# A new hand-written order for the engines of a fused attention and MLP kernel

## The chip, the cores and the metric

The kernel runs on one core of one Trainium2 chip. The core has five engines that run beside each other, each through its own list of instructions and in that list's order: PE (matrix products and their weight loads, PEld), DVE (vector arithmetic), ACT (functions by table, and copies), POOL (a second, slower vector engine, used here for casts and for issuing weight loads) and SP (which only issues transfers). Engines wait for each other by semaphores. Transfers between HBM and the on-chip memory are moved by 16 DMA engines; a transfer is issued by an engine's list and lands later.

The metric is the device time of one execution in microseconds. Three executions of the kernel before took 264.19, 266.99 and 267.23 us; the median is 266.99.

## The reference

Inputs are q, k and v of 4 batches, 8 heads, 768 positions and 64 columns, a list of 3 random key blocks for each of the 24 query blocks of 32, and the weights of an MLP.

```python
scores = q @ k.T / sqrt(64)                     # per batch and head, 768 x 768
mask   = |block_i - block_j| <= 1, or block_i or block_j is first or last,
         or block_j in sampled_blocks[block_i]
attn   = exp(where(mask, scores, -1e9) - max);  attn = attn / sum(attn)
x      = (attn @ v), heads side by side         # 3072 tokens x 512
h      = x @ w_in                               # 3072 x 2048
g      = h * sigmoid(beta * h)
out    = g @ w_out                              # 3072 x 512, float32
```

## The kernel before

**Attention.** Heads go in pairs (16 pairs, four in each batch), so that a pair's 2 x 64 columns fill 128 rows. Each pair's k, q and v are loaded as float32 into staging tiles `st` (the first pairs also into the not yet used `g` tiles), cast to float16 (`s16`, shown as `s` in the profile, and `va`), and k and q are transposed into `kX` and `qX`: for the first four pairs by PE and a copy, for the others by a transposing transfer that SP issues. The 768 queries of a pair are worked in two units of 256 and 512. A unit has several key steps: two 64-row matmuls for the two heads side by side give scores in PSUM (`sc`), ACT takes the exponential (`et`), DVE multiplies by the 0/1 mask. For the first four units PE adds the mask before the exponential instead. Then PE multiplies with v (`av`; a column of twos beside v gives twice the sum), DVE takes the reciprocal and normalizes into `xst`, and `xst` is transposed into `x`: by PE in the first eight units and the last, by a transposing transfer otherwise.

**MLP.** The tokens go in seven tiles: 256, five of 512, 256. For each of 16 chunks of the hidden width PE makes half of `h` (step kind `hp`; `x` is halved by the twos above), ACT `t = tanh(beta * h/2)` (`t_sb`), and DVE the product `(t + 1) * h/2` into `g`, which is h times the sigmoid. The second product is done plainly in the first tile. In the others it is done by seven half-sized products in place of eight; for that DVE makes sums of halves of `g` (`s`) and of `w_out` (`w_mix`), PE makes the seven products (`pr`), and ACT and DVE add them up in `osb`, from which SP stores to HBM.

**Tiles.** All tiles have fixed slots: 9 `st`, 7 `s16`, 15 `et`, 5 `xst`, 4 double PSUM banks, only 2 `osb` and 2 `g`. Whoever takes a slot waits for all that still use it.

**What sets the order.** The program first builds a list of steps (`Node`, numbered 0 to 1316 in the order of building), each with its engine or a choice of engines. The order in which they are emitted, and so each engine's list, is not found by a scheduler: it is written out in the string `STEPS` (line 43) and read by `in_steps` (line 163). A word such as `45G2` is step 45, on engine G (POOL; P is PE, A ACT, D DVE, S SP), in slot 2 of the tile that it takes. `824P2:823` emits step 824 crossed with step 823: both products are cut into upper and lower 64 rows, and PE runs the upper half of one beside the lower half of the other; the partner's own word later runs the other halves. `3x256V5` is three warm-up matmuls of 256 columns on zeros into bank 5. At the very start `emit_first` sets up constants and runs four warm-up matmuls of 512 columns.

A step on POOL that casts is also tied to the last DVE step ahead of it in the list (line 1034), so that it runs beside a DVE step that reads PSUM.

Steps that the texts below name: loads (`add_load`, line 497) of the first two pairs, 12, 16, 20, 24, 30, 34, 38 and 64, and of the next two, 44, 48, 54 and 58; their casts (`add_cast`, line 522); the mask steps 2, 3, 5, 7 and 9; the first scores, 91 to 95; step 310, the first `hp` of the second MLP tile; the stores (`add_store`, line 830) 395 to 398 of that tile; the transposes of attention tiles 593 to 723 and the first `hp` of the fourth tile, 724; the copy 566 into `osb` in the third tile.

Of the kernel before, what the change touches and what calls it, by code (L numbers as in the profile page):

```python
# [48 lines left out]
119P0 120A9 67D 98P 190P2 191A4 53D2 99D0 100D0 109P3 101P2 193P0 89P3 90D2 187P2 70P3 110P 102D  # L49
71D 194Ad 77G 78G 111Df 112D1 188Ae 196P0 199P1 197Aa 200A2 121P2 122P 123D1 124D4 195D 214P0  # L50
215A6 125P7 113P6 114D 202P2 203A5 126D 127P2 201D 198D 128A0 130P6 211P2 131A1 212A0 129D1 132D
189D 216D 136P3 145P7 146A1 137A3 133P2 134A5 213D 204D 142P0 143A4 147D 138D 144D 148P1 149A0
150D 135D 220P2 139P6 221Ab 140A2 151P7 217P2 152A6 141D 153D 192D 218Ac 219D 166P0 154P2 167A0
155A3 163P6 172P3 157P7 164A6 173A4 156D 168D 174D 226P2 165D 158A5 159D 160P2 227A3 169P3 223P0
161A1 228D 222D 170A3 171D 162D 224A8 252P2 225D 253A7 205P3 206P 207Df 208D2 246P0 254D 249P1
235G7 239G1 229P2:230 247A1 250Ad 261P3 262A9 230P 290P0 231D2 232D3 291Ab 181P23:175 258P3 255P2
256Ac 259A2 175P 209P1 182P 210A0 278P2 236S 243G2 248D 176P:183 237D5 263D 279Aa 281P0 284P3 240S
238S1 282A4 285A6 244S 270S3 183P 287P2 288Ae 177P 178P 184P 179A0 251D 257D 292D 260D 293P3 294A0
280D 241D2 358D 359D 360D 283D 289D 242S 265P0:264 185D1 286D 273S8 276S5 302S6 305S4 414P2 295D
362D 415A3 271G4 399P1 264P 266De 363D 267D4 405P3 296P2 297P 272S2 400A9 406Ac 268P3 298D7 299D0  # L60
269A 233P1 402P3 234A 300P0 403A2 411P1 408P2 274D0 308S0 422S7 425S1 412Aa 275S 301D 401D 310P0
322P7 331P2 319P1 311A6 364D 313P3 409Ab 332A0 303G3 320A1 323A4 314A5 277G2 423G5 309G0 328P5
329A3 306G6 361D 365D 316P6 312D1 407D 333D 321D 324D 315D 330D 317A1 413D 318D 430P0 431A1 404D
416D 432D 343P23:325 436P2 437A5 180S 304S3 186S 428S6 424S0 307S 325P 326A6 439P3 433P0 434A8
337P4 327D 435D 438D 410D 334P5 352P3 340P0 338A5 344A2 345D 335A0 353A1 346P1 354D 440A7 445P1
426G1 245G3 429G1 341A4 347A3 339D 336D 349P6 342D 446Ad 348D 442P2 366D0 447D 441D 443A4 444D
355P7 453P0 417P1 418P 456P2 454A0 356A6 350A5 419D3 420D1 427S 457Ac 459P0 460Ae 448P1:449 455D
357D 351D 369D 465P2 466A2 449P 468P3 469A6 462P0 463A8 375P4 450Dc 451D3 488P1 372P5:376 482P3
458D 467D 461D 464D 370D 470D 489A1 483A3 484D 367D 476P0 376P 477Aa 479P1 485P3 480Ab 373P 471P0
472P 486A4 586P1 587Ae 491P3 492Ad 374D1 377D 383P:380 473D3 474D0 583P0 594P1 595A5 608S8 380P  # L70
478D 381P:384 584Ac 481D 487D 368D 493D 490D 611S3 619P3 580P1 384P 620A6 609D4 378D 385A0 581A9
495P0:494 622P3 623A7 494P 616P1 379D 371D 617A0 614S5 630S0 633S2 612G6 634G5 389P 600P3 601A3
496D1 382D 497D2 386P:390 641P1 585D 596D 582D 631G2 638P0 642Aa 588D 390P 597P3 421S2 636S7 452S
652S1 475S 391D 610S1 644P1 387P 639A2 498S 653G0 621D 624D 388D 655S8 658S4 656G1 499P4 645A1
613S 598A8 395S 632S2 517P3 500A3 518A0 505P2 506A2 501D0 519D 589P0 590P 591D5 507D 392P4:508
592D4 646D 660P3 661A4 674S1 654S3 677S6 599D 675D3 618D 502P23:514 663P0 664Ab 508P 509A1 635S
396S 680S3 666P3 514P 665D 662D 510D 667Ad 515A2 503A0 526P0 527A6 511P1 393P 512A3 538P4 394A
539A4 678G4 516D 504D 688P3 682P1 689A9 528D 676S0 520P0 521A5 529P5 625P3 626P 683Ac 530A1 640D
540D 643D 602D 522D 627D5 513D 535P4 657S 628D0 536A2 696P1 699P0 603P3 604P 531D 684D 547D0 700Ae
605D2 537D 606D1 701D 679S 593S1 697A5 544P5 523P1 545A0 710P1 685P3 532P0 524A6 546D 711A6 647P2  # L80
659G3 615G0 668D 525D 541P2 533A4 534D 686A0 542A2 648P 702P0 637G2 669P3 670P 649Dh 650D3 703A3
808P2 543D 671D9 672D2 550D 687D 548D 698D 809A7 553P23:556 713P0 814P3 556P 557P:554 714Ad 815A4
716P2 717A8 690D 810D 551D 673S 398S 820P0 554P 555D1 681G1 704D 805P3 821A1 806Aa 691P2 692P
693D9 694D4 561P 817P3 818A0 706P2:705 828P0 558D 564P:562 829Ab 851S1 854S4 857S7 705P 559D 831P3
# [988 lines left out]
```

## Time and profile before

| what | us |
|---|---|
| median of three executions | 266.99 (264.19 to 267.23) |
| the profiled execution | 267.46 |
| its span, first to last instruction | 265.7 |
| PE busy | 254.4 |
| DVE busy | 227.4 |
| ACT busy | 213.1 |
| POOL busy | 41.7 |

The profile is of one execution. An engine's busy time counts its own instructions, not those that only wait or issue transfers. A row of the timeline starts with the start and the length in us and names engine, line, operation, what is written `<-` what is read, the shape and the number of instructions that the row merges; in brackets stand the idle time ahead of it and what ended that. Nearly all instructions have line L198, a helper that records them, so rows are told apart by their tiles. The chain of waits follows the end of the program back, at each step to what released it. The stage view gives for each stretch of time the busy time and number of instructions of each engine, the granted TensorE clock, the share of the DMA engines and what they moved.

### The profile page before, as it was taken

The numbers are of one execution on the slowest core, as the hardware profiler recorded it, in microseconds if no ns is written. First come the engines' busy times: TensorE is split into PE (matmuls) and PEld (weight loads), VectorE is DVE, ScalarE is ACT, GpSimd is POOL, SyncE is SP. The second block draws the span as 40 slices with busy tenths as digits, with TensorE's granted clock in tenths as the row PEclk, the third lists the DMA queues.
The fourth block names the chain that finished last, engine by engine and source line by source line (L and its number), as shares of the span: only waits on it lengthen the run. The fifth ranks groups of instructions, "written<-read, shape, count | busy, mean of one in ns | idle before, by whom it ended". The sixth has DMA issues, their size and how long they took to land.

```text
span 265.7 us, 8448 instructions
## 1 busy us (share of the span) xinstructions
PE 254.4 (96%) x3589; PEld 172.7 (65%) x3589; DVE 227.4 (86%) x442; ACT 213.1 (80%) x284; POOL 41.7 (16%) x60
## 2 busy tenths in 40 slices
PE   6999899999999999999989999989999999999994
PEld 1576575454357976558766557845757986568883
DVE  4475997989999997999988999999989997599581
ACT  3589999898999997999878999876689894574441
POOL 5183000017030051112104130060000000000000
PEclk9999999999999999999999999999999999999999
DMA  5899993899479449900965949640050100230042
GB/s 159 251 338 210 204 233 80 204 271 266 142 201 229 82 106 266 267 12 26 284 171 190 168 81 215 144 72 2 2 178 2 38 11 4 69 118 2 0 158 81
DMA packets 50153, 36.79 MB, mean 138 GB/s; under 512 B 29748, under 2 KB 46660, under 8 KB 50116
## 3 DMA queue, kind: packets, MB, share of 16 engines
q1 hardware_dynamic: 46368, 32.06, 47.2%
q0 software_dynamic: 3680, 4.19, 9.3%
q8 instruction: 28, 0.46, 0.7%
q14 instruction: 9, 0.07, 0.1%
q10 hardware_dynamic: 68, 0.01, 0.0%
HBM read 27.27 MB, written 6.29 MB: 126 GB/s over the span
## 4 chain that ended last, share of the span: by engine, by line
PE 72%; DVE 18%; ACT 4%; issue 2%; DMA 1%; SPq 0%; DVEq 0%; ACTq 0%
PE sc L198 72%; DVE et L198 6%; DVE g L198 6%; ACT et L198 3%; DVE s L198 1%; DMA out_dram<-osb 1%; DVE xst L198 1%; DVE w_out_sb L198 1%; DVE recip L198 1%; DVE kX L198 1%; DVE osb L198 1%; DVE va L198 1%; ACT t_sb L198 0%; ACT osb L198 0%; DVE w_mix L198 0%
## 5 line engine op out<-in xcount | busy, mean ns | idle before, releaser
L198 ACT ACTIVATE et<-sc 128x1024 f16<-128x1024 f32 x144 | 140.7, 1036 | 14.4 <-PE sc L198 11.8
L198 PE MATMUL sc<-x,w_in_sb 128*128 128x512 f16 (+2 forms) x496 | 92.8, 351 | 1.0 <-DVE g L198 1.0
L198 DVE TENSOR_TENSOR et<-et,mask 128x960 f16<-128x960 f16 x132 | 83.4, 668 | 0.7 <-ACT et L198 0.5
L198 ACT ACTIVATE t_sb<-sc,beta_c_sb 128x512 f16<-128x512 f32 (+1 forms) x112 | 65.4, 644 | 21.7 <-PE sc L198 16.7
L198 PEld LDWEIGHTS <-w_in_sb 128*128 128x128 f16 (+1 forms) x496 | 42.7, 97 | 38.3 <-issue 5.6
L198 DVE SCALAR_TENSOR_TENSOR g<-t_sb,sc 128x512 f16<-128x512 f16 (+1 forms) x112 | 63.1, 603 | 5.1 <-ACT t_sb L198 4.5
L198 PEld LDWEIGHTS <-g 64*128 64x128 f16 (+1 forms) x698 | 50.3, 96 | 16.7 <-issue 6.1
L198 PE MATMUL sc<-w_out_sb,g 64*128 64x256 f16 (+3 forms) x560 | 55.6, 280 | 1.6 <-ACT osb L198 1.6
L198 PE MATMUL sc<-qX,kX 64*128 64x512 f16 (+1 forms) x384 | 51.4, 329 | 0.8 <-DMA qX<-s 0.5
L198 PEld LDWEIGHTS <-et 64*128 64x128 f16 (+1 forms) x1608 | 41.0, 95 | 9.1 <-issue 3.2
L198 PE MATMUL sc<-va,et 64*128 64x65 f16 (+1 forms) x1608 | 44.1, 191 | 1.1 <-DVE xst L198 0.5
L198 POOL CAST s<-st 128x768 f16<-128x768 f32 (+1 forms) x23 | 20.4, 902 | 94.3 <-PE sc L198 48.6
L198 PEld LDWEIGHTS <-kX 64*128 64x128 f16 x384 | 19.9, 95 | 13.8 <-issue 8.2
L198 PEld LDWEIGHTS <-s 64*128 64x128 f16 (+1 forms) x320 | 22.6, 98 | 5.0 <-issue 1.6
L198 PE MATMUL sc<-w_mix,s 64*128 64x256 f16 (+1 forms) x272 | 24.3, 270 | 0.0
L198 DVE TENSOR_TENSOR xst<-sc,recip 128x256 f16<-128x256 f32 (+1 forms) x32 | 17.8, 556 | 0.8
L198 DVE TENSOR_TENSOR osb<-osb,sc 128x512 f32<-128x512 f32 (+2 forms) x19 | 11.8, 619 | 7.2 <-ACT osb L198 2.7
L198 ACT COPY osb<-sc 128x512 f32<-128x512 f32 (+3 forms) x19 | 10.0, 526 | 8.4 <-PE sc L198 6.0
L198 PE MATMUL sc<-w_mix,g 64*128 64x256 f16 (+3 forms) x128 | 15.3, 264 | 0.0
L198 DVE RECIPROCAL recip<-sc 128x4 f32<-128x4 f32 (+1 forms) x32 | 6.2, 193 | 7.8 <-PE sc L198 6.0
L198 POOL CAST va<-st 128x768 f16<-128x768 f32 x10 | 9.9, 1005 | 16.3 <-DVE g L198 10.2
L198 DVE TENSOR_TENSOR g<-g 128x1024 f16<-128x1024 f16 (+1 forms) x12 | 8.8, 743 | 0.0
(62 smaller groups left out, 97.2 us busy)
## 6 DMA issues: line engine op xcount, KB each, us to landing
out_dram<-osb SPq DMA_DIRECT2D x23, 256.0 KB, 2.5
st<-in_k_dram SPq DMA_DIRECT2D x12, 384.0 KB, 5.1
st<-in_q_dram SPq DMA_DIRECT2D x12, 384.0 KB, 4.0
st<-in_v_dram SPq DMA_DIRECT2D x12, 384.0 KB, 4.1
g<-in_v_dram SPq DMA_DIRECT2D x4, 384.0 KB, 7.0
w_in_sb<-in_moe_w_in_dram POOLq DMA_DIRECT2D x2, 512.0 KB, 7.8
w_in_sb<-in_moe_w_in_dram POOLq DMA_DIRECT2D x1, 1024.0 KB, 11.9
w_out_sb<-in_moe_w_out_dram POOLq DMA_DIRECT2D x2, 512.0 KB, 14.1
```

The costliest lines, as they stand in the source:

```text
L198: r = f(*a, **kw)
```

## The change

`STEPS` is replaced as a whole. Everything else in the file is the same: the same steps, tiles and slot counts. The new list has the same 1,317 numbered steps, without the two words for warm-up matmuls (`3V5` and `3x256V5`; the four in `emit_first` stay). In it differ: the order of the steps on each engine, above all up to step 310 and in the SP list; the slots; some choices of engine (casts: 17 on DVE and 36 on POOL, before 15 and 38; copies of mask, `x` and output products); and which products are crossed with which (36 pairs in both). The core of the diff, the beginning of the list:

```diff
 STEPS = """
-30S4 12S7 3V5 0D 1P6 2D 3A 6P0 8P7 3x256V5 9A 13G0 34S0 35G3 31G1 38S 44S0 16S0 24S 20S 48S1 54S2
-39D 45G2 25G 14P5 32P7 33D0 36P1 37D 40P6 15A1 41D 10P1 93P2 4P2 94Ab 7D 28S4 58S3 91P3 55G4 17D5
-5D 11D 18P0 19D 92A0 95P2 29G0 21D 46P1 22P0 79P1 23D 96Ac 80A6 49D6 26P0 72G 73G 74G 81P3 82A2
-42S5 64S0 68S8 69G0 75G 50P4 27D 47D2 51D 83P0 105P2 103P3 107P1 84A1 59D5 56P0 60P1 57D3 61D 52S6
-62S7 106A5 104A8 108A7 85P2 86P 117P0 118A1 115P3 87D4 76G 63G3 43D1 65D3 97P1 88D2 66P4 116A3
-...
-396S 680S3 666P3 514P 665D 662D 510D 667Ad 515A2 503A0 526P0 527A6 511P1 393P 512A3 538P4 394A
-...
-716P2 717A8 690D 810D 551D 673S 398S 820P0 554P 555D1 681G1 704D 805P3 821A1 806Aa 691P2 692P
-...
-549D 718D 562P 832A2 859P0 707Df 708D2 811P2 715D 712D 807D 552D 865P3 560D 565P 860A9 719P0 720P
-563A 866Ac 651S 629S 882S2 695S 885S3 567P 568P 709S 397S 721Da 722D0 607S 830D 812A6 566A0 843P3
-840P0 862P2 844A3 570P 571P 813D 861D 569D 822D 867D 572D 816D 819D 841Ae 863A5 723S 724P7 725A3
-727P4 728A4 852G2 855G1 883G4 888S6 726D1 729D 748P3 573P 845D 749A0 750D 837P3 824P2:823 834P0
-...
+0D 1P1 30S0 34S1 35G1 36P0 31G2 3A 38S 10P6 32P7 2A 39D 40P5 6P1 4P3 5A 12S3 16S4 33D0 37D 41D
+91P2 92Ae 7A 11D 17G5 24S 44S0 20S 13G1 64S4 95P3 21G 93P1 48S1 96A5 25D 54S2 58S3 45D6 14P4 22P0
+18P1 46P5 65D0 15D1 19D 23A 81P0 94A2 49D3 79P3 26P2 82A0 80Ac 72G 55G6 50P3 47D2 27D 83P0 51D
+105P1 107P3 59D1 28S4 29D0 84A1 60P4 42S5 52S6 68S8 73G 43G1 74G 69G4 75G 56P5 106Ad 108A8 103P0
+104A4 85P1 86P 57D3 61D 117P3 115P2 87Dg 88D0 66P3 53D2 67D 119P0 89P2 90D1 118A6 116Ab 97P3 98P
+...
+557P:554 717A9 820P3 680S2 396S 713P2 554P 821A0 805P0 714Ae 806A3 555D0 691P3 692P 712D 561P
+693D4 694D1 817P3 706P0:705 828P2 558D 718D 564P:562 851S3 651S 607S 854S4 398S 681G3 397S 673S
+552D 818A5 705P 831P3 629S 707Da 708D4 562P 829A8 859P0 832A4 860Ac 715D 559D 549D 560D 563A 811P2
+865P3 565P 719P0 720P 819D 721D2 722D2 857S6 882S0 695S 812A6 813D 810D 566A1 709S 866Ad 816D 567P
+568P 569D 822D 867D 885S5 723S 840P2 843P3 862P0 863A7 841Aa 844A9 570P 571P 861D 572D 807D 727P1
+724P0 728A6 725A1 748P3 573P 749A4 888S8 726D1 864D 729D 750D 837P3 838Ab 824P2:823 834P0 823P
+871P3 835Ae 872A1 757P3:574 868P0 574P 890P3 869A0 758A6 839D 845D 891A2 825D6 852D1 826D1 836D
+...
 """
```

The lines shown are the first five of both lists and those with the steps 396 to 398, 566, 607, 723 and 724. In the new one `16S4` gives the q load of the first pair a slot of its own (before `16S0`, the slot of `34S0`), `2A` puts the mask step 2 on ACT, and `398S` and `397S` stand ahead of `673S`.

More of the change, by code (lines that the diff above doesn't have):

```diff
@@ L49 @@
[L49 to L60, printed above, removed]
@@ new lines @@
+808P2 671D9 672D0 703Ac 809A1 704D 698D 687D 550D 690D 548D 551D 553P23:556 716P0 814P3 815A2 556P
+557P:554 717A9 820P3 680S2 396S 713P2 554P 821A0 805P0 714Ae 806A3 555D0 691P3 692P 712D 561P
[3 more added lines that the diff above has]
+568P 569D 822D 867D 885S5 723S 840P2 843P3 862P0 863A7 841Aa 844A9 570P 571P 861D 572D 807D 727P1
@@ L125 @@
+1308D 1309A 1310P 1311A 1314S 1312P6 1313D 1316S
 """
```

125 lines of the change are left out of this document (67 added, 58 removed).

## The prediction

> **What bounds the kernel now.** I read the page's busy times first, then the stages, then the chain that ended last.
>
> ```profile
> span 265.7 us, 8448 instructions
> ...
> PE 254.4 (96%) x3589; PEld 172.7 (65%) x3589; DVE 227.4 (86%) x442; ACT 213.1 (80%) x284; POOL 41.7 (16%) x60
> ...
> PE 72%; DVE 18%; ACT 4%; issue 2%; DMA 1%; SPq 0%; DVEq 0%; ACTq 0%
> ```
>
> PE (TensorE) is busy 96% of the span and holds 72% of the chain. An order can't shorten PE's own work much; it can remove waits. The profiled execution took 267.46 us, 1.76 us more than its span, and stands 0.5 us over the median of the runs, 266.99; I work on 267.46. The stages, cut where the chain changes engine:
>
> ```profile
> core 0: us, PE busy (x) PEld busy (x) DVE busy (x) ACT busy (x) POOL busy (x), PEclk, DMA share, GB/s
> 0.00:16.09 16.09, 13.70 (x93) 6.65 (x95) 8.34 (x31) 8.13 (x10) 6.77 (x21) 1.00 0.74 231
> 16.09:42.17 26.08, 24.71 (x388) 17.61 (x387) 20.71 (x51) 26.08 (x38) 6.35 (x10) 1.00 1.16 232
> 42.17:58.35 16.18, 15.12 (x258) 8.60 (x260) 14.06 (x27) 14.53 (x18) 1.61 (x2) 1.00 0.68 181
> 58.35:78.38 20.03, 19.02 (x143) 8.31 (x141) 19.98 (x34) 19.02 (x27) 7.13 (x8) 1.00 0.75 191
> 78.38:121.00 42.62, 42.62 (x705) 29.87 (x705) 40.70 (x75) 39.83 (x50) 7.81 (x9) 1.00 0.75 161
> 121.00:138.00 17.00, 15.80 (x283) 12.73 (x283) 15.62 (x32) 14.03 (x17) 1.59 (x2) 1.00 0.62 176
> 138.00:171.00 33.00, 33.00 (x537) 21.99 (x538) 30.20 (x52) 30.95 (x39) 6.01 (x6) 1.00 0.74 165
> 171.00:178.20 7.20, 6.52 (x75) 4.08 (x71) 7.20 (x11) 6.09 (x8) 3.26 (x4) 1.00 0.33 48
> 178.20:205.00 26.80, 26.80 (x408) 17.39 (x407) 25.15 (x44) 20.45 (x28) 1.19 (x1) 1.00 0.18 53
> ```
>
> So the bound moves. ACT has no idle time at all from 16.09 to 42.17 (26.08 of 26.08). DVE is the bound from 58.35 to 78.38 (19.98 of 20.03) and from 171 to 178.2 (7.20 of 7.20). PE is full from 78.38 to 121, from 138 to 171 and from 178.2 on. Only three places are open to an order: the start before 16.09, where ACT is busy 8.13 of 16.09 us; the stage 121 to 138, where PE stands 1.20 us and DVE 1.38; and the two DVE stretches.
>
> **The change part by part.** The same steps are issued, except for two. Against each other the two lists show: from the second MLP tile (PE step 310, at 58.83 us in this trace) to the last tile but one, PE's order is the same but for neighbours that change places; nearly everything new lies before it, in the SP queue, and in which of DVE, POOL and ACT does a copy.
>
> *Changes of row tiling on PE.* PE alternates between steps on two 64-row halves (scores, crossed pairs) and steps on 128 rows. I counted the changes in both lists: 94 before, 82 after. All 12 go before step 310 (50 against 38); behind it both have 44. The price:
>
> ```profile
> 68.34 4.49 PE L198 MATMUL sc<-x,w_in_sb 128*128 128x512 f16 x20
> 72.76 0.39 PE L198 MATMUL sc<-qX,kX 64*128 64x512 f16 x2
> 73.09 1.04 PE L198 MATMUL sc<-x,w_in_sb 128*128 128x512 f16 x4
> 74.06 0.39 PE L198 MATMUL sc<-qX,kX 64*128 64x512 f16 x2
> ```
>
> Twenty matmuls and one change take 72.76 − 68.34 = 4.42 us, four and one change 74.06 − 73.09 = 0.97. So four matmuls take (4.42 − 0.97)/4 = 0.86 and a change 0.11 us. Twelve are worth 1.3 us of PE time, but six of them lie before 28 us, where ACT and the loads set the pace, and the other six in 28 to 58, where PE holds about half of the chain. I count 0.4, with ends 0 and 1.3. Crossed pairs stay 36 (one pair of attention products fewer, one of output products more); at 0.11 per change saved or paid I count nothing more for them.
>
> *The start.* Two steps of warm-up matmuls go (three of 512 and three of 256 columns); the four at the very beginning stay. The q load of the first pair gets a staging slot of its own. Its cost before:
>
> ```profile
> 2.78 0.47 SPq L503 DMA_DIRECT2D g<-in_k_dram  x1
> 6.20 0.37 SPq L503 DMA_DIRECT2D st<-in_q_dram  x1
> ```
> ```profile
> 5.24 1.28 POOL L198 CAST s<-st 128x256 f16<-128x256 f32 x3 [2.17 <-DVE shut_qk L198]
> ```
> ```profile
> 6.40 0.82 PE L198 MATMUL sc<-g 128*128 128x256 f16 x3
> ```
> ```profile
> 9.66 1.02 ACT L198 ACTIVATE et<-sc 128x1024 f16<-128x1024 f32 x1 [1.82 <-PE sc L198]
> ...
> 16.09 4.75 ACT L198 ACTIVATE et<-sc 128x1024 f16<-128x1024 f32 x5 [0.23 <-PE sc L198]
> ```
>
> SP issued its fifth load at 2.78 and the sixth only at 6.20, because it wanted the slot that POOL's casts were reading; eleven more loads stood behind it. POOL's casts in turn started at 5.24, behind the DVE step that makes the mask (a POOL cast is tied to the DVE step ahead of it in the list). After, that mask step is on ACT, the casts are tied to the DVE step before, and SP passes eight loads at 0.51 us each (the rows' spacing) before the ninth waits for a slot; that one now waits for the cast of the sixth load, and eight loads stand behind it. So the loads of the first pair land up to 3 us sooner, those behind the ninth at about the old time. I expect the first exp near 7.9 instead of 9.66, an estimate: about 1 us from POOL's earlier casts (bounded by the q load, issued 0.51 sooner) and the 0.82 us of warm-up matmuls that stood ahead of the turns at 6.40. What counts is when ACT becomes dense, 16.09 before: the exps of the third pair need a load that was issued three places behind 6.20, near 7.7, and will be at about 8, and ACT has two mask copies more. Ends: 0 (the loads behind the ninth decide) and 1.8 (the whole shift of the first exp); I take 0.8, near the middle, since some of the old lateness was queueing on DVE and some the data.
>
> Both terms pass on: ACT is dense to 42, and DVE's stretch from 58.35 starts as soon as its inputs are there; its work up to 78.38 is the same within a cast. Sum at 78.38: −1.2 us, with ends 0 and −3.1. From there to 121 PE is full in both and keeps the gain.
>
> *The stores ahead of the transposes.*
>
> ```profile
> 133.91 3.32 DMA out_dram<-osb
> ```
> ```profile
> 133.91 0.57 SPq L834 DMA_DIRECT2D out_dram<-osb  x1
> 134.53 2.48 SPq L725 DMA_TRANSPOSE x<-xst  x2
> ```
> ```profile
> 137.30 0.59 ACT L198 COPY osb<-sc 128x512 f32<-128x512 f32 x1 [1.85 <-DMA out_dram<-osb]
> ```
> ```profile
> 137.94 1.25 PE L198 MATMUL sc<-w_out_sb,g 128*128 128x256 f16 x10 [1.20 <-ACT osb L198]
> ```
>
> There are two output buffers. ACT's copy at 137.30 waited for a store (step 397) to land, and PE stood 1.20 us behind the copy. The store was ready long before, but SP issued it at 133.91, behind transposes of attention tiles that were still being made. After, 397 and 398 stand before those: the two transposes still ahead of them take tiles whose products PE has finished by the start of this stage. The store then issues some 5 us sooner and lands, at the same 3.32 us, before ACT comes to it. What would be late next is the transpose that the next MLP tile waits for, the second of the row at 134.53: the two took 2.48 us, and the first of them now goes ahead with the stores, so the second comes 1.2 us sooner too. I count the whole 1.2 us that PE stood; ends 0 (DVE, which stood 1.38 in this stage, hides some other wait) and 1.2.
>
> *Copies that change engine.* DVE takes five casts of k and q from POOL between step 852 and step 1029 (the stages from 138 to 178) and gives one back; over the kernel it has two casts, two output copies and one x copy more and two mask copies less, ACT the reverse of the last three. What a cast costs on either side shows at 171:
>
> ```profile
> 171.72 1.02 DVE L198 CAST va<-st 128x768 f16<-128x768 f32 x2
> 172.66 2.42 DVE L198 TENSOR_TENSOR et<-et,mask 128x960 f16<-128x960 f16 x3
> 175.00 2.53 DVE L198 TENSOR_TENSOR g<-g 128x1024 f16<-128x1024 f16 x2
> ```
> ```profile
> 174.51 1.26 POOL L198 CAST va<-st 128x768 f16<-128x768 f32 x1
> ```
>
> Two DVE products beside POOL's casts took 2.53 us, 1.27 each, against the 0.57 of an undisturbed one (three et products with one of them disturbed took 2.42, so (2.42 − 1.27)/2). A cast on POOL that meets such a product costs DVE 0.7 us; a cast on DVE costs it about 0.5 (two in 1.02). So the moved casts are a wash: between −2.1 (three collisions in this stretch gone) and +2.0 (four casts in 138 to 171, where DVE has 33.00 − 30.20 = 2.8 us to spare). I count 0, hidden by those 2.8 us; without that cover it would cost its 2.0. The tail behind the last output product is the same in both lists.
>
> **Sum**: 267.46 − 0.4 − 0.8 − 1.2 = 265.06, so 265.0.
>
> **The rivals.**
>
> *Nothing is left of it*: DVE sets the end of more stages. It gains about 1.8 us of work between 138 and 178, directly behind the store's gain, and feeds the MLP products that PE takes at 178 to 205, where DVE is busy 25.15 of 26.80. If the spare time there is used up, the 1.2 goes again, and with the start at its lower end the time is 267. For it: DVE has the highest share behind PE. Against it: POOL's collisions go down at the same place.
>
> *Slower: PE stays at half rate longer.* The clock column of the stages shows 1.00 throughout, but the same two matmuls do not:
>
> ```profile
> 1.19 3.17 PE L198 MATMUL sc<-g 128*128 128x512 f16 x7 [1.19 <-DVE mask_blk L381]
> ```
> ```profile
> 11.68 0.42 PE L198 MATMUL sc<-shut_qk,onehot 64*128 64x256 f16 x2
> ...
> 13.50 0.27 PE L198 MATMUL sc<-shut_qk,onehot 64*128 64x256 f16 x2
> ```
> ```profile
> 13.50:20.00 6.50, 6.12 (x108) 4.91 (x102) 4.80 (x11) 5.85 (x7) 5.54 (x8) 1.00 1.09 337
> ```
>
> The two matmuls of 256 columns take 0.42 us at 11.68 and 0.27 at 13.50. Without the six warm-up matmuls PE's first 6 us are emptier. If the change comes as late as 20, the 6.1 us of PE work in 13.5 to 20 take up to twice the time; with 0.4 us of PE idle time to cover it, and half of the rest hidden behind ACT's 0.9 us per exp, that costs some 3 to 6 us: 265.0 + 4.5 = 269.5. It decides from a change at about 17 us; before that the gain at the start covers it. [...]
>
> *More than that is gained*: start at 1.8, row tiling at 1.3, collisions fewer: 267.46 − 1.8 − 1.3 − 1.2 − 1.2 = 262.
>
> *A transfer is late in a new place*: SP runs its queue in order, and one transpose that waits for its tile holds everything behind. A stall like the one at 137.3 costs 1.2 to 1.9 us; three to six new ones on top of an order that gains nothing else give 270 to 275.
>
> **How the numbers follow.** Forecast 265.0 (263 to 266.5): 0.47. Nothing left (266.5 to 268): 0.20. Slower by the rate (268 to 273): 0.13. More gained (260 to 263): 0.12. New late transfers (270 to 275): 0.08. The range 261.5 to 270.5 leaves out about 0.06 below and 0.13 above (half of the rate's case and nearly all of the transfers'). A measurement of this kernel tells about 2%, 5.3 us, from no change. Below 261.65 lies 0.06 of the chances, above 272.3 0.08, the rest between.
>
> **What would show it.** ACT's idle time before the copy behind the store (1.85 us) gone, and PE's 1.20; the first exp near 8 and ACT dense by about 15; the sixth load issued before 4; the same matmuls at 0.27 by 14 us; PE full behind 78. Wrong, if DVE's busy share in 138 to 205 rises to full, if exps have gaps behind 16, or if a store or transpose releases ACT or PE elsewhere.

## The result

| | before | after |
|---|---|---|
| median of 20 executions each, us | 266.82 | 264.23 |
| ratio, 95% interval | | 0.9916 (0.9889 to 0.9942) |
| the profiled execution, us | 267.46 | 263.51 |
| its span, us | 265.7 | 261.2 |

The changed kernel is 2.2 to 2.6 us faster (by the ratio, and by the difference of the medians; the interval of the ratio spans 1.5 to 3.0 us). The pair of profiled executions differs by 3.95 us. That is more than the change: the one of before stands 0.64 us over its median, the one of after 0.72 us under its own, and 3.95 − 0.64 − 0.72 = 2.59. A comparison of two traces therefore holds about 1.4 us that belong to the two executions. The experiments below were chosen to take the two apart.

The page of the kernel after, with its busy times and the shares of the chain that ended last:

```profile
span 261.2 us, 8344 instructions
...
PE 250.2 (96%) x3543; PEld 170.8 (65%) x3543; DVE 228.2 (87%) x445; ACT 210.7 (81%) x283; POOL 37.4 (14%) x58
...
PE 74%; ACT 11%; DVE 7%; issue 3%; DMA 2%; SPq 1%; POOL 0%; DVEq 0%
```

DVE holds 7% of the chain where it held 18%, ACT 11% where it held 4%, and PE's busy share is what it was. The stage view of the kernel after, cut at the places that answer to those of before:

```profile
core 0: us, PE busy (x) PEld busy (x) DVE busy (x) ACT busy (x) POOL busy (x), PEclk, DMA share, GB/s
0.00:11.35 11.35, 8.28 (x52) 3.83 (x53) 5.12 (x25) 5.50 (x10) 4.04 (x17) 1.00 0.79 246
11.35:40.00 28.65, 26.40 (x424) 19.49 (x425) 23.73 (x55) 28.65 (x42) 8.69 (x13) 1.00 1.12 222
...
119.00:134.00 15.00, 15.00 (x280) 12.44 (x276) 14.19 (x30) 13.86 (x16) 1.55 (x2) 1.00 0.69 156
134.00:167.00 33.00, 33.00 (x530) 21.20 (x529) 31.65 (x56) 29.94 (x39) 3.30 (x4) 1.00 0.65 153
167.00:174.20 7.20, 7.20 (x98) 4.93 (x91) 6.93 (x13) 6.36 (x8) 0.36 (x1) 1.00 0.48 130
174.20:201.00 26.80, 26.80 (x409) 17.55 (x408) 25.69 (x44) 21.60 (x29) 1.30 (x2) 1.00 0.28 58
```

ACT is now without a gap from 11.35 on (in the trace of before from 16.09). PE has no idle time in 119 to 134, where it stood 1.20 us, nor in 167 to 174.2, where it had worked 6.52 of 7.20. The timeline of the kernel after at the start, SP first, then ACT, then PE:

```profile
1.75 0.97 SPq L503 DMA_DIRECT2D st<-in_k_dram  x2
2.77 0.47 SPq L503 DMA_DIRECT2D st<-in_q_dram  x1
3.28 0.47 SPq L503 DMA_DIRECT2D st<-in_k_dram  x1
...
4.82 0.47 SPq L503 DMA_DIRECT2D st<-in_q_dram  x1
```
```profile
7.83 1.02 ACT L198 ACTIVATE et<-sc 128x1024 f16<-128x1024 f32 x1 [0.49 <-PE sc L198]
...
11.35 11.12 ACT L198 ACTIVATE et<-sc 128x1024 f16<-128x1024 f32 x12
```
```profile
6.01 0.81 PE L198 MATMUL sc<-mask_q,onehot 24*128 24x384 f16 x2
...
9.08 0.41 PE L198 MATMUL sc<-qX,kX 64*128 64x256 f16 x2
9.42 0.28 PE L198 MATMUL sc<-identity,s 128*128 128x128 f16 x2
...
11.50 0.29 PE L198 MATMUL sc<-shut_qk,onehot 64*128 64x256 f16 x2 [0.79 <-ACT kX L198]
...
41.71 0.49 PE L198 MATMUL sc<-va,et 64*128 64x65 f16 x20 [1.49 <-issue]
```

SP's sixth load is issued at 3.28 (before 6.20), and the ninth, step 64, at 4.82: it waited for nothing. The q load 16, the sixth of the old list, is the fifth of the new one and goes at 2.77. The first exp stands at 7.83. Two matmuls of 256 columns take 0.41 at 9.08 and 0.29 at 11.50, and such pairs start 0.21 us apart up to 9.08 and 0.11 apart from 11.50 on. So the rate doubles, in this trace by 9.42, some 3.8 us sooner than in the trace of before, where it did so at 13.2 to 13.4; the next section shows that this place moves from one execution to the next. One row is new and bad: PE stands 1.49 us in the middle of an attention product, and the trace names no releaser for it. And the place of the store, SP, ACT and PE:

```profile
122.82 0.89 SPq L834 DMA_DIRECT2D out_dram<-osb  x2
```
```profile
132.66 0.61 ACT L198 COPY osb<-sc 128x512 f32<-128x512 f32 x1
```
```profile
134.12 0.82 PE L198 MATMUL sc<-qX,kX 64*128 64x512 f16 x6
134.87 1.92 PE L198 MATMUL sc<-w_out_sb,g 128*128 128x256 f16 x16
```

Both stores go at 122.82, and neither the copy nor the product behind it waits any more.

### The profile page after: what moved, and what is told of

Read it like the earlier page. It is cut to its first block, busy times and chain, and to the rows that moved or that the text cites. A ratio compares the mean times of both kernels' runs of the same rounds, so it can differ in the third digit from the quotient of the medians.

```text
span 261.2 us, 8344 instructions
## 1 busy us (share of the span) xinstructions
PE 250.2 (96%) x3543; PEld 170.8 (65%) x3543; DVE 228.2 (87%) x445; ACT 210.7 (81%) x283; POOL 37.4 (14%) x58
## 4 chain that ended last, share of the span: by engine, by line
PE 74%; ACT 11%; DVE 7%; issue 3%; DMA 2%; SPq 1%; POOL 0%; DVEq 0%
PE sc L198 74%; ACT et L198 8%; DVE et L198 4%; ACT t_sb L198 3%; DMA st<-in_k_dram 2%; SPq L503 1%; DVE w_mix L198 1%; DVE xst L198 1%; DVE osb L198 0%; DVE recip L198 0%; DVE x L198 0%; POOL s L198 0%; ACT kX L198 0%; DVE g L198 0%; DVE kX L198 0%
## 5 line engine op out<-in xcount | busy, mean ns | idle before, releaser
L198 ACT ACTIVATE et<-sc 128x1024 f16<-128x1024 f32 x144 | 139.4, 1043 | 13.3 <-PE sc L198 10.9
L198 PE MATMUL sc<-x,w_in_sb 128*128 128x512 f16 (+2 forms) x496 | 92.4, 351 | 0.6 <-DVE g L198 0.5
L198 DVE TENSOR_TENSOR et<-et,mask 128x960 f16<-128x960 f16 x132 | 84.1, 671 | 0.7 <-ACT et L198 0.6
L198 ACT ACTIVATE t_sb<-sc,beta_c_sb 128x512 f16<-128x512 f32 (+1 forms) x112 | 65.0, 640 | 22.9 <-PE sc L198 20.4
L198 DVE SCALAR_TENSOR_TENSOR g<-t_sb,sc 128x512 f16<-128x512 f16 (+1 forms) x112 | 63.9, 605 | 4.9 <-ACT t_sb L198 4.4
L198 PEld LDWEIGHTS <-w_in_sb 128*128 128x128 f16 (+1 forms) x496 | 42.8, 97 | 36.8 <-issue 4.2
L198 PEld LDWEIGHTS <-g 64*128 64x128 f16 (+1 forms) x700 | 49.0, 96 | 14.4 <-issue 2.8
L198 PE MATMUL sc<-w_out_sb,g 64*128 64x256 f16 (+3 forms) x568 | 55.9, 281 | 0.0
L198 PE MATMUL sc<-qX,kX 64*128 64x512 f16 (+1 forms) x384 | 51.1, 329 | 1.2 <-DVE qX L198 0.4
L198 PEld LDWEIGHTS <-et 64*128 64x128 f16 (+1 forms) x1560 | 41.6, 96 | 10.0 <-issue 3.5
L198 PE MATMUL sc<-va,et 64*128 64x65 f16 (+1 forms) x1560 | 44.6, 191 | 1.6 <-issue 1.5
L198 PEld LDWEIGHTS <-kX 64*128 64x128 f16 x384 | 19.5, 95 | 14.0 <-issue 8.0
L198 PEld LDWEIGHTS <-s 64*128 64x128 f16 (+1 forms) x320 | 21.5, 96 | 5.7 <-POOL s L198 1.3
L198 PE MATMUL sc<-w_mix,s 64*128 64x256 f16 (+1 forms) x272 | 23.8, 270 | 0.0
L198 POOL CAST s<-st 128x768 f16<-128x768 f32 (+1 forms) x21 | 16.8, 817 | 46.2 <-PE sc L198 22.4
L198 POOL CAST va<-st 128x768 f16<-128x768 f32 x11 | 9.5, 866 | 69.5 <-DVE va L198 20.2
L198 DVE TENSOR_TENSOR xst<-sc,recip 128x256 f16<-128x256 f32 (+1 forms) x32 | 17.6, 554 | 0.7
L198 DVE TENSOR_TENSOR osb<-osb,sc 128x512 f32<-128x512 f32 (+2 forms) x19 | 11.7, 618 | 5.4 <-PE sc L198 4.9
L198 PE MATMUL sc<-w_mix,g 64*128 64x256 f16 (+3 forms) x128 | 15.4, 264 | 0.0
L198 DVE RECIPROCAL recip<-sc 128x4 f32<-128x4 f32 (+1 forms) x32 | 6.2, 192 | 8.7 <-PE sc L198 8.5
L198 ACT COPY osb<-sc 128x512 f32<-128x512 f32 (+3 forms) x17 | 8.8, 517 | 5.5 <-PE sc L198 4.5
L198 DVE CAST s<-st 128x768 f16<-128x768 f32 (+2 forms) x11 | 5.5, 501 | 3.7 <-DMA st<-in_k_dram 3.2
```

Of the source, the lines that this page charges most:

```text
L198: r = f(*a, **kw)
```

## Where the time went: the same steps in fourteen executions

All kernels of this study have the same numbered steps, so the start of one step can be compared over all their traces. The table gives, in us, how much later than in the trace of before a step starts (minus is sooner); 191 is an exp on ACT, the others are steps of PE. In brackets stands the start in the trace of before. The last column is the ratio of times to before, with its 95% interval. The rows are explained with their experiments.

| kernel | 191 (22.60) | 448 (78.38) | 567 (134.08) | 837 (143.39) | 790 (172.37) | 1021 (187.17) | time |
|---|---|---|---|---|---|---|---|
| after | −2.21 | −2.25 | −1.80 | −3.20 | −3.06 | −3.98 | 0.9916 (0.9889 to 0.9942) |
| after, again (e9) | −2.56 | −2.45 | −1.95 | −3.35 | −3.21 | −3.78 | 0.9925 (0.9891 to 0.9959) |
| after, casts back (e4) | −2.61 | −2.70 | −2.21 | −3.61 | −3.18 | −4.11 | 0.9910 (0.9868 to 0.9953) |
| after, one slot back (e11) | −0.47 | −0.90 | −0.12 | −1.52 | −1.38 | −2.17 | 1.0020 (0.9992 to 1.0048) |
| after, casts tied (e12) | −2.31 | −0.23 | +0.32 | −1.09 | −0.95 | −1.87 | 0.9923 (0.9887 to 0.9960) |
| after, 78 early (e8) | −2.39 | −2.96 | −2.46 | −3.86 | −3.72 | −4.35 | 0.9840 (0.9796 to 0.9885) |
| after, 76 to 78 early (e10) | −2.29 | −2.96 | −1.86 | −3.26 | −3.12 | −3.80 | 0.9862 (0.9827 to 0.9897) |
| new to 310, then old (e2) | −2.59 | −2.44 | −2.49 | −3.00 | −3.09 | −3.00 | 0.9952 (0.9922 to 0.9982) |
| old to 310, then new (e3) | −1.45 | −0.89 | −0.61 | −2.01 | −1.15 | −1.99 | 0.9978 (0.9945 to 1.0012) |
| before, store early (e1) | −1.44 | −0.79 | −0.78 | −0.64 | −0.55 | −0.46 | 0.9986 (0.9959 to 1.0013) |
| before, store and 607 early (e6) | −1.32 | −0.66 | −0.25 | −1.63 | −1.36 | −2.20 | 1.0005 (0.9966 to 1.0043) |
| before, other banks (e5) | −2.49 | −1.86 | −1.85 | −1.71 | −1.80 | −1.90 | 0.9973 (0.9939 to 1.0007) |
| before, no warm-up (e7) | −0.63 | +0.22 | +1.18 | +0.64 | +0.92 | +0.08 | 1.0006 (0.9974 to 1.0037) |

The rounds of e5, e6, e7 and e8 ran on another chip, on which the kernel before took 268.00 us in place of 266.45 to 266.82: times of those four kernels are to be read by their ratios.

Read it by columns. Up to step 448 the rows e1, e5 and e6 have the very list of before, and yet they stand at −0.79, −1.86 and −0.66: four executions of one list lie 1.9 us apart there, and the trace of before is the latest of them. The four executions of the new first part with its slot and its weight loads as they are (after, e9, e4, e2) lie between −2.25 and −2.70. The means are −0.83 and −2.46, so the new first part is worth 1.6 us at 448, and not the 2.25 that the pair of traces shows.

The old list's starts go with the moment at which PE reaches its full rate. Two matmuls of 256 columns go from 0.42 to 0.27 us at 13.4 in before and at 9.8 in e1. In e6 they do so at 11.1, after an earlier fast stretch (two mask products take 0.48 us at 5.59, in before 0.79). In e5 they take 0.28 from 7.8 on, where the first scores start. The four stand at 448 in about that order (0, −0.79, −0.66, −1.86). In e1 ACT is dense from the first exp on:

```profile
9.21 0.42 PE L196 MATMUL sc<-qX,kX 64*128 64x256 f16 x2
...
9.96 0.27 PE L196 MATMUL sc<-qX,kX 64*128 64x256 f16 x2
```
```profile
9.67 18.07 ACT L196 ACTIVATE et<-sc 128x1024 f16<-128x1024 f32 x19 [1.83 <-PE sc L196]
```

So the 16.09 at which ACT becomes dense in before is that of a late execution, and not of its list. In the traces of the new first part the full rate comes between 8.6 and 11.3 us. Against e1 alone, which is at the full rate at about the same time, the new first part is worth 1.7 us at 448. One more thing limits what the table can say: the profiled executions of e2, e5, e6 and e11 were the fastest of their twelve, that of before was slower than 15 of its 20.

## The experiments

### Is it the first part or the rest?

The new list up to step 310 with the old order behind it, and the other way round; where the two halves met, 27 and 31 slots had to be renamed.

```diff
 e2: STEPS = new list up to and with 310P0, then all other words in the old list's order
 e3: STEPS = old list up to and with 310P0, then all other words in the new list's order
```

> The new list up to step 310, and behind it the old list's order (27 slots renamed so that they fit). Theory from the two traces (start, row tiling and order up to step 310): step 430 starts about 2.2 us sooner than before, the later stages run as before, the end is 2.2 us sooner: about 264.6. By the prediction's own terms (0.4 and 0.8) it is 1.2 us: 265.6. Rival: the gain up to 448 in the trace belongs to what stands behind step 310 in the new list (at 310 itself the shift was only 0.78), then 266.0.

> The old list up to step 310, and behind it the new list's order (31 slots renamed). Theory: the store's 1.2 us and the 0.9 us of the stretch 167 to 201 and 0.45 us of the tail remain, 2.5 us less than before: 264.3. By the prediction's terms only the store: 265.6. Rival (all of it was won up to step 310): 266.8, as before. If the two halves add up, this run and the one with the new head give together the difference between the kernels.

The times are 265.85 and 266.12 us beside 266.73 of before: 1.3 and 0.6 us less by the ratios, 1.9 together, against 2.4 for the changed kernel with its casts back (e4), which ran in the same rounds. Within the intervals the halves add up, and the larger lies in the first. The 264.6 that the trace of after had suggested for the first part was too low, the 264.3 for the rest as well.

### One slot at the start

The q load 16 goes back into the staging slot of load 34.

```diff
-... 38S 10P6 32P7 2A 39D 40P5 6P1 4P3 5A 12S3 16S4 33D0 ...
+... 38S 10P6 32P7 2A 39D 40P5 6P1 4P3 5A 12S3 16S1 33D0 ...
```

> The changed kernel with the q load 16 of the first pair in staging slot 1, that of load 34, as the kernel before had them in one slot. Theory of the prediction: SP stands at this load until POOL's cast 35 has read the slot (about 4.5 us), so it and the eleven loads behind it issue some 1 to 1.5 us later; the first exp stays near 7.9 or goes to 8.5, ACT becomes dense at 12 to 13 instead of 11.4, and the time is 0.5 to 1 us longer. Rival (the loads land late because the DMA engines are full, not because they are issued late): the same exps within 0.3 us and the same time.

266.87 us, against 264.20 of the changed kernel in the same rounds: 1.0020 of before instead of 0.9925, which is 0.95% or 2.5 us (1.4 to 3.7 by the two intervals). One digit holds as much as the whole change. The whole new first part in front of the old rest (e2) gave 1.3 us (0.5 to 2.1), so the two intervals only overlap. The timeline of this kernel, SP and ACT (where an edit shortened the list by two lines, L503 is L501 and L198 is L196):

```profile
1.75 0.97 SPq L501 DMA_DIRECT2D st<-in_k_dram  x2
4.22 0.37 SPq L501 DMA_DIRECT2D st<-in_q_dram  x1
```
```profile
11.18 2.86 ACT L196 ACTIVATE et<-sc 128x1024 f16<-128x1024 f32 x3
15.20 3.81 ACT L196 ACTIVATE et<-sc 128x1024 f16<-128x1024 f32 x4 [1.16 <-PE sc L196]
19.40 2.85 ACT L196 ACTIVATE et<-sc 128x1024 f16<-128x1024 f32 x3 [0.38 <-PE sc L196]
```

SP stands 1.45 us (4.22 instead of 2.77), and the twelve loads behind it are 0.9 to 1.4 us later. The first exp does not care (7.58 in this trace); the price is paid from 14 us on, where ACT runs dry twice, for 1.54 us together. At step 191 the kernel is 1.7 us behind after, and at 448 it stands at −0.90, in the middle of the old lists. PE reaches its full rate at about 10 us in this trace, as in e1 (9.8), which stands at −0.79. So everything else in the new first part, the fewer changes of row tiling among it, shows no gain at 448.

### POOL's casts behind the mask step

```diff
-0D 1P1 30S0 34S1 35G1 36P0 31G2 3A 38S 10P6 32P7 2A 39D ...
+0D 1P1 30S0 34S1 2D 35G1 36P0 31G2 3A 38S 10P6 32P7 39D ...
```

> The changed kernel with the mask step 2 on DVE and ahead of POOL's casts 35 and 31 in the list, as in the kernel before, so that these casts are tied to it. Theory of the prediction (POOL's first casts waited for the mask): POOL's first cast starts near 4.5 to 5.2 instead of 3.8, the first exp comes 0.5 to 1.2 us later than 7.83, and the exps behind 16 us and the time are 0.3 to 0.8 us later. Rival: the data, not the casts, decide; the exps from the third on stand within 0.2 us of the changed kernel.

```profile
4.28 0.74 POOL L196 CAST s<-st 128x256 f16<-128x256 f32 x2 [1.22 <-DVE shut_qk L196]
```
```profile
7.91 1.02 ACT L196 ACTIVATE et<-sc 128x1024 f16<-128x1024 f32 x1 [0.49 <-PE sc L196]
```

The casts come 0.47 us later (4.28 for 3.81) and the first exp 0.08 (7.91 for 7.83); at 191 nothing is left of it (−2.31 for −2.21 and −2.56), and the time is 0.9923 for 0.9925. The tie costs nothing that is measured. Why this execution falls back by 2 us between 191 and 448 is told below, with PE's idle time at 40.

### The store, alone and with a transpose

```diff
 e1:
-... 673S 398S 820P0 ... 709S 397S 721Da 722D0 607S 830D ...
+... 673S 398S 397S 820P0 ... 709S 721Da 722D0 607S 830D ...
 e6:
-... 673S 398S 820P0 ... 709S 397S 721Da 722D0 607S 830D ...
+... 673S 398S 397S 607S 820P0 ... 709S 721Da 722D0 830D ...
```

> The kernel before with one word moved: store 397 goes into SP's list right behind store 398, ahead of the loads and transposes 651, 629, 695 and 709. Theory of the prediction (the store held ACT's copy 566 and through it PE): the store issues near 125.5 instead of 133.91, the copy's 1.85 us and PE's 1.20 us of waiting are gone, and the time is 1.2 us less, about 265.6 against 266.8. Rival (nothing is left of it): the waits go, but step 798 and the end stand within 0.4 us of before, because DVE takes the time back between 138 and 205. A store that only pushes the transposes back would make PE step 724 late instead, and show an x transpose as the releaser.

> The kernel before with store 397 and transpose 607 right behind store 398 in SP's list (in the first experiment 607 had stayed behind). Theory: what gave the store's 1.26 us back there was that transpose 723 stood behind 607; with 607 ahead 723 goes as soon as its tile is made (DVE step 722), PE does not stand 1.39 us inside 724, and the gain of 1.2 us is still there at step 837 and at 1021: 265.5 against 266.7. Rival (the two loads or 695 and 709 hold 723 as well, or DVE takes it back): at 837 the shift is the same as at 567.

In both, step 570 stands 1.3 us better than 567 (e1 −2.05 behind −0.78, e6 −1.52 behind −0.25), as in the changed kernel (−3.06 behind −1.80): the wait for the store in the trace of before is worth 1.26 us at its place every time. In other traces that still have the wait PE stands there for 1.35 us (e5), 0.69 (e2) and 0.66 (e7), so 1.2 is toward its upper end. What becomes of the gain differs. The timeline of e1 (store alone), SP and PE:

```profile
133.11 3.75 SPq L723 DMA_TRANSPOSE x<-xst  x3
```
```profile
137.65 0.81 PE L196 MATMUL sc<-x,w_in_sb 128*128 128x512 f16 x3
139.84 2.10 PE L196 MATMUL sc<-x,w_in_sb 128*128 128x512 f16 x9 [1.39 <-DMA st<-in_v_dram]
```

The last three transposes (709, 607, 723) still go in one block, the last of them ends at 136.86, and PE stands 1.39 us inside step 724, behind its first three matmuls. The trace names a load as the releaser; the load was issued directly behind the transposes. In e6, with 607 ahead:

```profile
136.42 1.92 PE L196 MATMUL sc<-w_out_sb,g 128*128 128x256 f16 x16
138.18 2.77 PE L196 MATMUL sc<-x,w_in_sb 128*128 128x512 f16 x12
```

Step 724 runs through, and the gain stands at 837 (−1.63) and at the end. So the traces bear the theory out in both halves: the store alone gives its gain back four steps later, store and transpose together keep it. The times do not: 0.9986 for e1, which gave its gain back, and 1.0005 (0.9966 to 1.0043) for e6, where 1.2 us would be 0.9955, outside the interval. The profiled execution of e6 was the fastest of its twelve (264.97 against a median of 267.35). Together with e3 (0.6 us less, 0.3 more to 1.5 less by its interval) the times allow the store 0 to 1 us, not surely more. The shorter wait of e2 and e7 is one reason; what takes the rest back in the other executions isn't seen in any trace, and stays open.

### Five casts back on POOL

```diff
-... 852D1 ... 883D2 ... 889G2 ... 914D4 ... 1026D6 ... 1029D5 ...
+... 852G1 ... 883G2 ... 889D2 ... 914G4 ... 1026G6 ... 1029G5 ...
```

> The changed kernel with the casts 852, 883, 914, 1026 and 1029 back on POOL and 889 back on DVE, as before the change; the order is the new one. The prediction's term 4 (a wash): within 0.4 us of the changed kernel, 264.2. Theory from the trace after (the unforeseen 0.9 us between 167 and 201 come from POOL casts that no longer slow DVE's products): 0.9 us slower, 265.1, and DVE products of 1.2 us near 170. Rival (DVE has too little to spare and the casts on it cost time): up to 2 us faster, 262.2.

264.04 us, against 264.23 and 264.20 of the changed kernel: the engine of these casts makes no difference that is measured (the interval of the seven executions is 1.1 us to either side). The gain between 790 and 1021 stays as well (−3.18 to −4.11, 0.93 us), though POOL casts again beside DVE's products; one of them collides. POOL and DVE of this kernel:

```profile
170.98 1.19 POOL L196 CAST s<-st 128x768 f16<-128x768 f32 x1 [4.70 <-DVE et L196]
```
```profile
171.40 1.31 DVE L196 TENSOR_TENSOR g<-g 128x1024 f16<-128x1024 f16 x1
```

So the theory that moved casts had given the 0.9 us fell.

### Other banks for four first products

In the trace of before PE waits here, between 790 and 1021, for bank 2, which DVE must empty:

```profile
178.18 4.05 PE L198 MATMUL sc<-x,w_in_sb 128*128 128x512 f16 x18 [0.68 <-DVE g L198]
```

```diff
-... 933P2 ... 942P1 924P4 ... 951P3 ... 1021P1:1020 ... 1059P2 ...
+... 933P3 ... 942P4 924P2 ... 951P1 ... 1021P2:1020 ... 1059P1 ...
```

> The kernel before with other PSUM banks for four first products of the sixth MLP tile: 933 in bank 3 (was 2), 942 in 4 (was 1), 924 in 2 (was 4), 951 in 1 (was 3); steps 1021 and 1059 then change their double banks too. Theory (the 0.9 us that the changed kernel gains between 790 and 1021 is PE's wait for bank 2, which DVE empties with 923 only at 178.13): PE has no idle time ahead of 933, and the shift against before at step 1021 is 0.7 us better than at step 790; the time is 0.7 less, 266.0 against 266.7. Rival (DVE is the bound there, whatever the bank): the wait moves to a later first product or to 792, and nothing is gained at 1021.

```profile
172.84 7.94 PE L196 MATMUL sc<-x,w_in_sb 128*128 128x512 f16 x36
181.47 1.02 PE L196 MATMUL sc<-x,w_in_sb 128*128 128x512 f16 x4 [0.69 <-DVE g L196]
```

The wait at 933 is gone and stands, with 0.69 us for 0.68, in front of a later first product; between 790 and 1021 nothing is gained (−1.80 to −1.90). The rival holds: DVE is the bound in this stretch, not the bank. And e6 and e7, whose list is that of before at this place, gain 0.84 us each here without any edit. Their DVE rows tell why. That of e6, to be read beside the two rows that the prediction quotes of before (three products in 2.42, two in 2.53):

```profile
171.03 1.79 DVE L196 TENSOR_TENSOR et<-et,mask 128x960 f16<-128x960 f16 x3
172.73 2.53 DVE L196 TENSOR_TENSOR g<-g 128x1024 f16<-128x1024 f16 x2
```

Three products in 1.79 are undisturbed. In before, e1, e2 and e5 POOL's casts meet three of DVE's five products, in e6 and e7 two, and one collision (2.42 − 1.79 = 0.63 us) goes with the difference between a PE that waits 0.7 to 0.9 us and one that doesn't. The same list falls on either side from one execution to the next; the new order, in all eight traces that have it, stands on the good side, with 0.6 to 0.9 us from 790 to 1021. The rows give the size of a meeting and not its mechanism: a product takes 0.57 to 0.60 us alone, from start to start (after, from 171.43 to 172.60), and 1.2 to 1.3 beside a cast (before two in 2.53, e4 one in 1.31); the cast takes 0.83 us by itself and 1.19 beside the product (both e4).

### Without the warm-up

```diff
-30S4 12S7 3V5 0D 1P6 2D 3A 6P0 8P7 3x256V5 9A 13G0 ...
+30S4 12S7 0D 1P6 2D 3A 6P0 8P7 9A 13G0 ...
```

> The kernel before without its two steps of warm-up matmuls (three of 512 and three of 256 columns). The rival of the slower rate: PE goes to full rate later than the 13.2 us of before, at 17 or behind, and the time is 1 to 4 us longer, 268 to 271. [...]

```profile
13.38 0.35 PE L196 MATMUL sc<-shut_qk,onehot 64*128 64x256 f16 x2
13.57 0.27 PE L196 MATMUL sc<-qX,kX 64*128 64x256 f16 x2
```

The rate changes at 13.4 us, as in before (13.2 to 13.5), and the time is 1.0006 of before. In the trace of after it had changed by 9.42. The rival of the slower rate fell. What sets the moment of the change is not shown. In the trace of after PE works without a gap from 5.47 on and is at the full rate at 9.42, 3.95 us later; in e7 it had worked without a gap since 6.06, 7.3 us, and in before since 5.67, 7.5 us. One length of steady work doesn't give all three.

### PE's idle time at 40 us, and a faster version

```diff
 e8:
-... 76G 77G 235G2 78G 253A6 ...
+... 76G 77G 78G 235G2 253A6 ...
 e10:
-... 8P4 193P3 187P0 9D 63G3 109P2 ... 246P2 76G 77G 235G2 78G 253A6 ...
+... 8P4 193P3 187P0 9D 76G 63G3 77G 78G 109P2 ... 246P2 235G2 253A6 ...
```

> The changed kernel with the last load of w_out (78) ahead of the copy 235 in POOL's list, so that it is issued near 23.4 us and not at 31.48. Theory (PE's 1.49 us of idle time at 40.2, which the trace puts down to no releaser, is a fetch of its instructions that waits behind this load, the DMA share being 1.06 in 38 to 44): the idle time falls to 0.5 or less as in the kernel before, and the time to 263.2 against 264.2. Rival (the wait is PE's own and has nothing to do with the load): still 1.5 us at step 230, 264.2. If the early load takes the place of q, k or v loads, ACT gets gaps between 20 and 38 and it is slower.

> The changed kernel with all three late loads of w_out earlier in POOL's list: 76 ahead of the cast 63, and 77 and 78 right behind it (before: all behind step 206). Theory (PE's idle time at step 230 is a fetch behind full DMA engines): the loads issue by 21.5 us instead of 24.1, the idle time at 40 falls from the 0.96 of the run with 78 alone moved to 0.5 or less, and the time to about 0.5 under that run, 1.5 to 2 us under the changed kernel. Rival (the wait is not one for the DMA engines): 1 to 1.5 us of idle time stay at step 230, and the time is that of the changed kernel. If the weights now take the place of the loads of v, ACT shows gaps between 18 and 30.

> The changed kernel unaltered, beside the next three and beside the kernel before. Expected 0.992 of before as in its first measurement, so 2 to 2.5 us less. Its profile shows how far one execution of it lies from another: if the 0.9 us between 790 and 1021 belongs to the new order, it is there again; PE's idle time at 40 is expected again, at 1 to 1.8 us.

The changed kernel again (e9) does as expected: 0.9925, 0.57 us gained between 790 and 1021, and 1.63 us of idle time at 40. With the loads moved the times are 262.70 and 262.82 us, the two fastest kernels of the study; e10 ran in the same rounds as e9, whose median is 264.20, and is 1.4 us under it. The executions also lie closer together: 262.56 to 263.01 in e8 and 261.66 to 263.32 in e10 (six each), 262.68 to 266.62 in e9 (twelve). PE's rows at this place for before, e12 and e8, to be read beside the 1.49 of after (e9 has 1.63, e10 0.87):

```profile
42.61 0.55 PE L198 MATMUL sc<-va,et 64*128 64x65 f16 x24 [0.48 <-issue]
```
```profile
42.58 0.49 PE L196 MATMUL sc<-va,et 64*128 64x65 f16 x20 [2.45 <-issue]
```
```profile
41.00 0.49 PE L196 MATMUL sc<-va,et 64*128 64x65 f16 x20 [0.96 <-issue]
```

The idle time has no releaser, and lies in the middle of a step whose inputs were all there. It stands at this place in all fourteen traces: 0.48 to 1.15 us in the six with the old first part, 1.08 to 2.45 in the six with the new one and its late load (0.48 and 2.45 are the ends, before and e12), 0.96 and 0.87 with the loads moved. It doesn't go with the share of the DMA engines in 38 to 44 alone: e7 stands 1.15 us at a share of 0.62, e4 1.44 at 1.44, e12 2.45 at 1.31. It goes with a transfer. In every trace one packet of 16 KB of the queue that the profile calls q8 instruction lands here, and PE goes on 1.3 to 1.7 us behind its landing. In e12 the packet goes from 40.19 to 41.16, and PE, out of work since 40.12, goes on at 42.58; in e8 it goes from 38.65 to 39.65, and PE, out of work at 40.03, goes on at 41.00. The DMA view of these two, e12 from 40.1 to 41.2 and e8 from 38.6 to 39.7, has that one packet:

```profile
q8 instruction: 1, 0.02, 5.5%
```
```profile
q8 instruction: 1, 0.02, 5.7%
```

The second stop near 57 us that five traces of the old first part have comes 1.3 to 1.5 us behind such a packet too. In before and after the other packets of q8 (28 and 27 on their pages) land without a stop: two waits of PE in before and one in after have no releaser. What the traces show is this order in time; that the packet brings PE's own instructions, and that PE waits for them, is the author's reading of the queue's name. In the changed kernel the last load of `w_out` was issued at 31.48 and lands in this stage; in e8 the three issue from 21.77 to 24.1. That this load is what holds the packet back is argued, while the remedy is measured. The expected 0.5 us or less was not reached, and moving 76 and 77 as well brought nothing more.

At step 448 the traces of e8 and e10 gained 0.5 us (−2.96 against −2.46), the time of e10 1.4. The rest goes with the clock in these kernels. Of the 50 executions of the changed kernel (after and e9) and of e4 and e12, 17 have a mean granted clock of 0.992 to 0.994, and in each of the four rows these are 1.7 to 2.4 us longer in the mean than the others (0.998 to 1.00); of the twelve of e8 and e10 none has. A low clock doesn't always come with a longer time: of the kernel before, in the rounds of e9, 12 of 27 executions stand at 0.987 to 0.994, and they are 0.4 us shorter in the mean. The profiled execution of e12 is one of the 17. Behind its 2.45 us of idle time the clock is granted at 0.73 in 44 to 50, and eight matmuls take 1.96 us that take 1.04 in e9:

```profile
42.97 1.04 PE L198 MATMUL sc<-w_out_sb,g 64*128 64x512 f16 x8
```
```profile
44.05 1.96 PE L196 MATMUL sc<-w_out_sb,g 64*128 64x512 f16 x8
...
44.00:50.00 6.00, 6.00 (x44) 2.98 (x44) 4.90 (x10) 3.94 (x5) 1.76 (x2) 0.73 0.55 153
```

In this execution the longest stop (2.45 us) and the low clock (0.73) stand one behind the other; that the one brings the other, and that the earlier load avoids it, is the author's reading of this one execution and of the counts above. Of the other traces only that of e6, on the old list, has a low clock (0.994), and of e2's twelve executions, which have the late load too, only one has. The 2 us that e12 loses between 191 and 448 lie here: 0.9 us where PE goes on (42.58 for 41.71 in after) and 1.6 in the slow matmuls behind it (the products at 50.40 stand at 47.93 in after). They are not put down to the edit: 9 of the 32 executions of after and e9 have such a clock as well. The slot's 2.5 us holds some of it too: eight of e11's twelve executions have a clock of 0.985 to 0.994, and among those at 0.998 or more e11 is 2.0 us longer than e9 (four executions against eight).

## Why the prediction was right, point by point

The forecast was 265.0 us (263 to 266.5 for its own case), measured are 264.23. The number was right, its composition was not.

- **Changes of row tiling, 0.4**: not found. With one slot put back, all the rest of the new first part stands at −0.90 at 448, among four executions of the old list (0 to −1.86, mean −0.83). A term of 0.4 is smaller than what two executions differ by there, and the price of 0.11 us for a change was not measured by itself.
- **The start, 0.8**: mis-sized; it measured 1.6 us in the traces at 448 and 2.5 in the time (1.4 to 3.7), at the upper end of 1.8 and over it. The step that failed is "that one now waits for the cast of the sixth load, and eight loads stand behind it". Load 64 is in the same slot as load 16, but it fills the other columns of that tile, and SP issued it at 4.82 without a wait. (The q load, which the prediction calls the sixth, is the fifth in the new list.) So the gain of the sixth load (3.28 for 6.20) was passed on down the queue (the ninth 4.82 for 7.64), not to three loads only, and ACT was dense at 11.35 instead of "by about 15". The 16.09 that this was counted from belonged to one late execution: in e1 the old list has ACT dense from 9.67. Two reasons given there were wrong as well: POOL's earlier casts were not what moved the first exp (e12: 0.08 us), and the slot did not either (e11: 7.58). What brought the first exp from 9.66 to 7.83 was not isolated: with the old list it stands at 9.67 in e1, 8.80 in e6 and 8.52 in e5, and without the warm-up (e7) at 8.54.
- **The stores, 1.2**: right in the traces, at the place (1.26 us) and in what would be late next: with the transpose left behind, PE stood in step 724 (e1), with it ahead it didn't (e6). The times don't confirm the size; they allow 0 to 1 us, and the wait itself was 0.66 to 1.35 us from one trace to the next.
- **Copies that change engine, 0**: right as far as measured (e4).
- **Not foreseen, for**: 0.6 to 0.9 us between 790 and 1021, from DVE's order there, in executions where the old list has three collisions. The prediction had this stretch as DVE's, with "three collisions in this stretch gone" as the lower end of the term, and counted nothing.
- **Not foreseen, against**: PE's idle time at 40, 1.49 us where the trace of before has 0.48. That pair overstates it: the old list has a second such stop near 57 us in five of its six traces, and the two together take 0.88 to 1.62 us (1.28 in the mean), against 1.08 to 2.45 (1.63 in the mean) in the new. The delayed `w_out` load was in the diff, and the DMA share of 1.16 in 16 to 42 in the stages; neither was followed to PE.
- **The rivals**: nothing left by DVE fell (PE is busy 33.00 of 33.00 from 134 to 167 and 26.80 of 26.80 from 174.2 to 201). The slower rate fell (e7, and the full rate by 9.42 in the trace of after). A late transfer is what e1 shows, 1.39 us, but not the changed kernel. More gained (262) came true at the start alone.

Added up from the table, the traces give 1.6 at 448, 1.3 for the store and 0.6 to 0.9 behind 790, 3.5 to 3.8 us; the times give 2.2 to 2.6. Part of the difference is the clock: among executions at 0.998 or more, e9 takes 263.75 us in the mean and the kernel before 266.65 in the same rounds, 2.9 us less. The rest is that part of the store's and of the last gain which the times don't bear out.

## What to carry to other kernels

In a queue that works in order, look for the first entry that must wait and count what stands behind it: here one staging slot held eleven loads (twelve in e11) and was worth as much as the whole change, give or take 1.2 us, and whether a transfer waited was decided by the columns that it writes, not by the slot's number alone (load 64, in the slot of load 16, went at 4.82 without a wait). A store that is moved ahead keeps its gain only if the transfer that the next consumer needs comes ahead with it: without it PE stood 1.39 us in step 724 (e1), with it not at all (e6). And before an effect of a microsecond is read from two traces, compare the same list in several executions: here they lay 1.9 us apart by step 448, in about the order in which PE reached its full rate, and one collision of POOL and DVE went with 0.84 us.

## What the runs showed of the hardware

PE stood for 0.48 to 2.45 us near 40 us without any releaser, and in all fourteen traces it went on 1.3 to 1.7 us behind the landing of a 16 KB packet of the queue that the page calls q8 instruction (1.3 in before, 1.5 in after). That it waited for its own instructions is read from this order in time and from the queue's name. A kernel that issues its last weight load 8 us sooner stood 0.96 us there (e8) in place of 1.49 and 1.63 (after and e9), and none of the twelve executions of e8 and e10 had a low clock, where 17 of 50 had. They lie within 0.5 us (e8) and 1.7 us (e10) of each other, six each, where the twelve of e9 had lain 4 us apart. The page of after lists two queues of this kind:

```profile
q8 instruction: 27, 0.44, 0.7%
q14 instruction: 9, 0.07, 0.1%
```

The packet behind which PE goes on is one of q8; the last packet of q14 lands 1.1 us ahead of that moment in before, 2.8 in after and 4.0 in e12, so its distance is not the same from trace to trace.
